# Fewer small VectorE operations in routing and list updates, and a changed instruction plan, in a recurrence followed by a mixture of experts

## The chip, the cores and the metric

The kernel runs on one core of one Trainium2 chip. The metric is the device time of one execution in microseconds: 506.29 us as the median of three runs (505.67 to 507.88). Engines are named as the profile names them: PE (TensorE matmuls), PEld (its weight loads), DVE (VectorE), ACT (ScalarE), POOL (GpSimd), SP (SyncE, which issues DMAs). L1247 is line 1247 of the kernel before.

## The reference, cut to what matters

```
x, f_logit: (4, 5056, 256) f32          # 20224 tokens of 256 values
f = lb + (1 - lb) * sigmoid(f_logit);  h_t = f_t * h_(t-1) + (1 - f_t) * x_t     # along each of 4 sequences
y = all h_t, as 20224 rows
logits = cos(y, expert_emb) / tau       # 8 experts, norms with + 1e-6
e = argmax(logits);  g = softmax(logits)[e]
out[row] = g * (relu(y[row] @ w1[e]) @ w2[e])        # w1: 256 x 1024, w2: 1024 x 256 per expert
```

## The kernel before, in words

**Routing.** The tokens go through in 40 chunks of 512 (the last is half). For each chunk PE transposes the gate input (`F_`, L667) and x (`X_`, L701) into eight [128, 512] banks of PSUM, ACT makes the gates (L678, L684), DVE multiplies (L709) and scans along time (L725). ACT squares the result (L737). From chunk 12 on ACT also writes a bf16 copy `hbf` (L743), which two transposing DMAs bring into token order (`Yt`); before that PE does it (L761). Two chunks make a group (22 groups; the first and last two have one chunk). Per group PE computes logits and squared norms (L819, L823), and DVE finds the best expert of every token, its slot, and its gate (`route_`, `gate_`: some two dozen operations on 8 to 64 columns). POOL then scatters the group's rows, 128 at a time, into a scratch tensor in DRAM that is sorted by expert (L1015, 158 scatters).

**List updates.** After 11 of the groups `update_` turns the counts per expert into a list of tiles of 256 rows of one expert: for each tile of the list the row at which it starts and the place of its expert's weights in SBUF (`tbl`).

**Expert tiles.** SP reads the start of a tile from `tbl` and loads its rows transposed from the scratch (`ys`, L1207), after all scatters of the groups that the list covers. PE runs 16 matmuls of the first layer (L1247), ACT and DVE apply relu (L1265, L1270), PE runs 16 matmuls of the second layer (L1284), ACT and DVE scale by the gate into `osb` (L1299, L1303), and POOL scatters two times 128 rows to the output (L1309). Of 86 tiles that may be needed 83 run always; the last three are skipped when the list is empty there. The weights of all experts (16 DMAs of POOL with a cast, L647) have to be in SBUF before the first tile.

**What sets the order.** `Prog.op` records every operation with what it reads, writes and costs, and `Prog.schedule` replays the engines with these costs, always giving an engine the waiting operation of the lowest `prio`, and writes a fixed order for each of the five engines and the bank of each PSUM use. The priority is the chunk for routing, 10000 + j for tile j, and -1 (ahead of everything) for a tile's evictions and output scatters. `SHADOW` and `PACE` are constants of this replay: a paced scatter on POOL gets a wait for the last PE step that ends at least `PACE` ns before the scatter's planned start.

Of the kernel before, what the change touches and what calls it, by code (L numbers as in the profile page):

```python
# [34 lines left out]
class Prog:  # L35
# [8 lines left out]
    SHADOW = 2500  # L44
    DMA_FIX = 1900
    PACE = 900.0
    DMA_RATE = 400.0

# [65 lines left out]

    def schedule(self, first, caps):
# [24 lines left out]
        bus, scat = 0.0, -1e9  # L140
# [7 lines left out]
        def lag(d):  # L148
            return d.end + self.LAT[d.eng] + self.PAD

# [5 lines left out]
        while True:  # L156
# [16 lines left out]
            if avail[e]:  # L173
                p, i, o = heapq.heappop(avail[e])
            else:
                t, p, i, o = heapq.heappop(wait[e])
            new = [h for h in o.hold if h.b is None]
# [19 lines left out]
            if o.dma is not None:  # L197
                bus = max(bus, free[e]) + o.nbytes / self.DMA_RATE
                o.end = max(bus, free[e]) + self.DMA_FIX
            else:  # L200
                o.end = free[e] + self.LAG[e]
                if e == "pe":
                    o.end = max(o.end, scat + self.SHADOW)
            if e == "pe" and not o.quiet:
                steps.append((free[e], o))
            if e == "pool" and o.dma is not None:
                scat = s
# [121 lines left out]
def bass_hgrn_recurrence__then__cosine_router_kernel(  # L329
# [20 lines left out]
    T = 256  # L350
# [17 lines left out]
    with ExitStack() as es:  # L368
# [19 lines left out]
        base17 = sb("base17", [P, 17])  # L388
        ex17 = sb("ex17", [P, 17])
# [30 lines left out]
        nr3 = [sb(f"nr3{q}", [P, 16]) for q in range(R2)]  # L420
        rs = [sb(f"rs{q}", [P, 16]) for q in range(R2)]
# [4 lines left out]
        NU = 12  # L426
        cnt = [sb(f"cnt{q}", [P, 8]) for q in range(2)]
        qn = [sb(f"qn{q}", [P, 8]) for q in range(2)]
        seg = sb("seg", [P, 16])
        cum = [sb(f"cum{q}", [P, 17]) for q in range(2)]  # L430
        cmp_ = sb("cmp", [P, 18])
        val = sb("val", [P, 17])
        t17 = sb("t17", [P, 17])
        t17b = sb("t17b", [P, 17])
        acc = [sb(f"acc{q}", [P, 2]) for q in range(2)]
        dac = sb("dac", [P, 2])
# [11 lines left out]
        NO = 4  # L448
# [3 lines left out]


        def pool(fn, cost=400, **k):
            return op("pool", fn, cost, **k)
# [12 lines left out]


# [21 lines left out]

        load(0)
        sp(lambda e: e.dma_start(embt[:], moe_expert_emb[:]), 8192, "ld0", w=["embt"])
# [13 lines left out]
        def iota(dst, pattern, base=0, mult=0, w=()):  # L507
# [3 lines left out]

        pool(lambda e: e.memset(ident[:], 0.0), w=["ident"])
# [10 lines left out]
            2, r=["lb0", "lb1"], w=["cs0"],  # L523
# [3 lines left out]
            2, r=["lb0", "lb1"], w=["cs1"],  # L527
# [13 lines left out]
        pool(lambda e: e.memset(onesb[:], 1.0), w=["onesb"])  # L541
# [10 lines left out]
        def late_constants():  # L552
            iota(iscr[:, 0:1], [[0, 1]], mult=1, w=["iscr"])
            pool(lambda e: e.tensor_copy(iop[:], iscr[:, 0:1]), r=["iscr"], w=["iop"])
            iota(iscr[:, 0:16], [[0, 2], [1, 8]], w=["iscr"])
            pool(
                lambda e: e.tensor_scalar(
                    ex17[:, 0:16], iscr[:, 0:16], float(2 * WE), 0.0, op0=ALU.mult, op1=ALU.add
                ),
                r=["iscr"], w=["ex17"],  # L560
            )
            pool(lambda e: e.memset(ex17[:, 16:17], 0.0), w=["ex17"])

            iota(iscr[:, 0:16], [[0, 2], [CB, 8]], w=["iscr"])
            pool(lambda e: e.tensor_copy(base17[:, 0:16], iscr[:, 0:16]), r=["iscr"], w=["base17"])
            pool(
                lambda e: e.tensor_scalar(
                    base17[:, 16:17], iop[:], -1.0, float(NULLROW // T), op0=ALU.mult, op1=ALU.add
                ),
                r=["iop"], w=["base17"],  # L570
# [3 lines left out]
                    nio[:], base17[:, 0:8], float(T), 0.0, op0=ALU.mult, op1=ALU.add  # L574
                ),
                r=["base17"], w=["nio"],
            )
            pool(lambda e: e.memset(nulr[:], 0.0), w=["nulr"])
# [6 lines left out]
            pool(lambda e: e.memset(acc[0][:], 0.0), w=[("acc", 0)])  # L585
            pool(lambda e: e.memset(qn[0][:], 0.0), w=[("qn", 0)])
            pool(lambda e: e.memset(cum[0][:], 0.0), w=[("cum", 0)])
            pool(lambda e: e.memset(seg[:], 1.0), w=["seg"])
# [12 lines left out]
        ]  # L601
        ew = lambda i: embw[:, D + i : D + i + 1]
# [3 lines left out]
        dve(lambda e: e.reciprocal(ew(2), ew(1)), 1, r=["ew1"], w=["ew2"])  # L606
        dve(lambda e: e.tensor_tensor(ew(3), ew(0), ew(2), ALU.mult), 1, r=["ew0", "ew2"], w=["ew3"])
        dve(lambda e: e.tensor_tensor(ew(4), ew(1), ew(3), ALU.add), 1, r=["ew1", "ew3"], w=["ew4"])
        dve(
            lambda e: e.tensor_scalar(ew(5), ew(4), 0.5, 1e-6, op0=ALU.mult, op1=ALU.add),  # L610
            1, r=["ew4"], w=["ew5"],
        )
# [20 lines left out]
        )  # L633


        def wload(i, c):
# [6 lines left out]
            else:  # L643
# [3 lines left out]
                "pool", lambda e: e.dma_start(dst, src), 1000, w=[("w", i)], dma=f"w{i}",  # L647
# [84 lines left out]
        def Y_(c):  # L732
# [8 lines left out]
            if c >= CT and nb == 4:  # L741
# [12 lines left out]
                return  # L754
            for hf in range(nb // 2):
# [23 lines left out]
                )  # L779

# [141 lines left out]
        def gate_(bi):  # L922
# [502 lines left out]
```

## Time and profile before

| | |
|---|---|
| median of 3 runs | 506.29 us |
| the profiled execution: its own time, its span | 503.07 us, 500.9 us |
| PE busy | 449.8 us, 90% |
| PEld busy | 383.7 us, 77% |
| DVE busy | 371.5 us, 74% |
| POOL busy | 337.1 us, 67% |
| ACT busy | 328.1 us, 65% |
| DMA queues q1 (SP's), q0 (POOL's) | 47.2% and 30.9% of 16 engines |
| TensorE clock granted, mean of the span | 0.971 |

Busy shares are means over two very different stages: routing with tiles between its chunks, until about 297 us, and tiles alone after it. They are read stage by stage. An instruction's duration reaches past the start of the next one on the same engine, so the cost of a small one is the distance between starts, not its duration. [...]

### The profile page before, as it was taken

Reading aid. Unit: us, or ns where it says so; the run is one execution under the profiler, and the core shown is the slowest. Engines: PE = TensorE matmul, PEld = TensorE weight load, DVE = VectorE, ACT = ScalarE, POOL = GpSimd, SP = SyncE. Lnnn points to the kernel's source line nnn. Section 1 sums busy time; section 2 is a strip of 40 time slices with the busy share of each in tenths; the row PEclk is TensorE's granted clock in tenths of the full one; section 3 lists DMA queues with packets and bytes.
Section 4 is the critical chain, followed back from the end, with each engine's and each line's share of the span. In section 5 each row is a group of like instructions: output and inputs, shape, how many; then the busy total and the mean of one; then the engine's idle time right before and its main releaser. Section 6 shows DMA issues by size and latency. Waiting matters only on the chain.

```text
span 500.9 us, 12508 instructions
## 1 busy us (share of the span) xinstructions
PE 449.8 (90%) x4009; PEld 383.7 (77%) x4009; DVE 371.5 (74%) x1202; ACT 328.1 (65%) x549; POOL 337.1 (67%) x404
## 2 busy tenths in 40 slices
PE   4878786587898999999799999999999999999994
PEld 3556564565787877877677688999999999999993
DVE  6799999576998999999899997454545545455552
ACT  6789887466787988988798844444445444454442
POOL 5144376775677677777777777777777777755565
PEclk9989989598998999999999999999999999999999
DMA  8999999789999999999998544656554456645411
GB/s 264 318 299 322 316 314 296 165 193 282 245 241 275 303 262 283 244 297 288 268 306 182 129 109 128 173 131 135 127 139 125 114 129 140 157 120 116 117 34 42
DMA packets 127584, 101.77 MB, mean 203 GB/s; under 512 B 104532, under 2 KB 106591, under 8 KB 127520
## 3 DMA queue, kind: packets, MB, share of 16 engines
q1 hardware_dynamic: 111104, 60.70, 47.2%
q0 software_dynamic: 16416, 40.27, 30.9%
q8 instruction: 34, 0.56, 0.5%
q14 instruction: 30, 0.25, 0.2%
HBM read 58.38 MB, written 34.01 MB: 184 GB/s over the span
## 4 chain that ended last, share of the span: by engine, by line
PE 57%; DVE 19%; DMA 10%; ACT 8%; issue 5%; SPq 1%; POOL 1%; ACTq 0%
PE bank L1247 23%; PE bank L1284 22%; DMA Yt<-hbf 6%; DVE hb L725 5%; PE bank L819 4%; PE bank L667 3%; DVE bank L709 3%; PE bank L701 3%; DVE hT L1270 3%; ACT fg L684 2%; DMA fin<-in_f_logit_dram 2%; ACT th L678 2%; DVE osb L1303 1%; DMA XsScratch<-Yt,sli 1%; ACT sq L737 1%
## 5 line engine op out<-in xcount | busy, mean ns | idle before, releaser
L1309 POOL DMA_INDIRECT out_dram<-osb,xm x166 | 164.6, 991 | 67.2 <-issue 30.5
L1015 POOL DMA_INDIRECT XsScratch<-Yt,sli x158 | 152.2, 963 | 58.9 <-issue 25.4
L1247 PE MATMUL bank<-ys,wall 128*128 128x256 bf16 x1328 | 167.1, 276 | 7.3 <-DMA ys<-XsScratch 5.0
L1284 PE MATMUL bank<-wall,hT 128*128 x1328 | 165.5, 273 | 3.9 <-ACT hT L1265 3.4
L1270 DVE TENSOR_SCALAR hT<-bank 128x512 bf16<-128x512 f32 x166 | 112.7, 685 | 74.9 <-PE bank L1247 72.0
L1247 PEld LDWEIGHTS bank<-ys,wall 128*128 x1328 | 149.1, 144 | 13.4 <-issue 5.6
L1284 PEld LDWEIGHTS bank<-wall,hT 128*128 128x128 bf16 x1328 | 128.5, 98 | 23.0 <-ACT hT L1265 4.2
L1265 ACT ACTIVATE hT<-bank 128x512 bf16<-128x512 f32 x166 | 98.1, 595 | 69.8 <-PE bank L1247 67.9
L725 DVE TENSOR_TENSOR_SCAN hb<-fg,hb,bank 128x512 f32<-128x512 f32 (+4 forms) x78 | 96.4, 1239 | 0.2
L1299 ACT ACTIVATE osb<-bank,xm 128x256 f32<-128x256 f32 x83 | 39.1, 471 | 47.8 <-PE bank L1284 42.3
L701 PE MATMUL bank<-ident,xin 128*128 128x128 f32 x316 | 53.3, 295 | 12.8 <-ACT fg L684 10.4
L684 ACT ACTIVATE fg<-th,cs 128x512 f32<-128x512 f32 (+1 forms) x80 | 64.0, 810 | 1.1
L1303 DVE TENSOR_SCALAR osb<-bank,xm 128x256 f32<-128x256 f32 x83 | 39.7, 478 | 31.8 <-ACT osb L1299 25.2
L709 DVE SCALAR_TENSOR_TENSOR bank<-fg,bank 128x512 f32<-128x512 f32 (+1 forms) x80 | 54.7, 686 | 7.3 <-PE bank L701 5.8
L667 PE MATMUL bank<-ident,fin 128*128 128x128 f32 x316 | 51.9, 294 | 6.4 <-DMA fin<-in_f_logit_dram 5.5
L701 PEld LDWEIGHTS bank<-ident,xin 128*128 128x128 f32 x316 | 38.2, 149 | 23.3 <-ACT fg L684 17.0
L678 ACT ACTIVATE th<-bank 128x512 f32<-128x512 f32 (+1 forms) x80 | 45.7, 587 | 8.0 <-PE bank L667 7.8
L667 PEld LDWEIGHTS bank<-ident,fin 128*128 128x128 f32 x316 | 40.0, 153 | 14.4 <-issue 7.0
L737 ACT ACTIVATE sq<-hb 128x1024 f32<-128x1024 f32 (+1 forms) x40 | 41.8, 1045 | 13.1 <-DVE hb L725 13.0
L819 PE MATMUL bank<-hb,eT 128*8 128x512 f32 (+1 forms) x160 | 41.8, 601 | 6.5 <-ACT th L678 3.3
L823 PE MATMUL bank<-sq,onesf 128*1 128x512 f32 (+1 forms) x160 | 41.7, 600 | 0.0
L743 ACT ACTIVATE hbf<-hb 128x1024 bf16<-128x1024 f32 x27 | 28.3, 1050 | 9.7 <-DMA Yt<-hbf 9.7
(114 smaller groups left out, 301.3 us busy)
## 6 DMA issues: line engine op xcount, KB each, us to landing
fin<-in_f_logit_dram SPq DMA_DIRECT2D x39, 512.0 KB
xin<-in_x_dram SPq DMA_DIRECT2D x39, 512.0 KB
wall<-in_moe_w_dram POOLq DMA_DIRECT2D x16, 512.0 KB, 10.0
out_dram<-osb,xm POOLq DMA_INDIRECT x166
XsScratch<-Yt,sli POOLq DMA_INDIRECT x158
ys<-XsScratch SPq DMA_TRANSPOSE x83
xm<-XsScratch SPq DMA_DIRECT2D x83, 2.0 KB
XsScratch<-nulr SPq DMA_DIRECT2D x8, 136.0 KB
```

The source lines that it names most:

```text
L667: i = e.transpose(bank[h.b][:, b : nb * P : nb], fin[q][:, b, dh * P : (dh + 1) * P], ident[:],)
L684: lambda e, dh=dh: e.activation(fg[c % 2][:, dh, 0:n], th[dh][:, 0:n], AF.Identity, bias=cs[:, dh, 0:1], scale=cs[:, dh, 1:2],),
L701: i = e.transpose(bank[h.b][:, b : nb * P : nb], xin[q][:, b, dh * P : (dh + 1) * P], ident[:],)
L709: lambda e, dh=dh, h=h: e.scalar_tensor_tensor(out=bank[h.b][:, 0:n], in0=fg[c % 2][:, dh, 0:n], scalar=1.0, in1=bank[h.b][:, 0:n], op0=AL ...
L725: lambda e, dh=dh, s0=s0, s1=s1, init=init, h=h: e.tensor_tensor_scan(hb[c % NH][:, dh, s0:s1], fg[c % 2][:, dh, s0:s1], bank[h.b][:, s0:s ...
L819: i = e.matmul(bank[hl.b][32 * k_ : 32 * k_ + 8, 0:n], eT[:, kt, :], hb[c % NH][:, kt, 0:n], start=(kt == 0), stop=(kt == DT - 1),)
L1015: lambda e, j=o + j, i=o + k_ * 4 + b: e.indirect_dma_start(out=Xs[:, :], out_offset=bass.IndirectOffsetOnAxis(ap=sli[y][:, j : j + 1], axis=0
L1247: i = e.matmul(bank[hh[f // 2].b][:, (f % 2) * T : (f % 2 + 1) * T], wall[:, bass.ds(a1[j][(4 * mp + f) * DT + kt] - WA - WREV, 2 * FT * P ...
L1265: lambda e, o=o, h=h: e.activation(o, bank[h.b][:], AF.Relu), 512,
L1270: lambda e, o=o, h=h: e.tensor_scalar(o, bank[h.b][:], 0.0, None, op0=ALU.max),
L1284: i = e.matmul(po(s), hT[qh][:, kf, s * P : (s + 1) * P], wall[:, bass.ds(a2[j][kf] - WA, 2 * D)].bitcast(BF16), start=(kf == 0 and s == 0 ...
L1309: lambda e, s=s: e.indirect_dma_start(out=out[:, :], out_offset=bass.IndirectOffsetOnAxis(ap=xm[qx][:, s, 1:2], axis=0), in_=osb[qo][:, s, :],
```

## The change

It rewrites two blocks of small DVE operations, changes the planner's constants and rules, and adds matmuls of ones.

- **List update.** The list entry of a tile is a sum over experts. Before, the update computed the segments, their running sum, two comparisons' difference, and two masked sums (17 operations, 22 in the last update). Now the running ends of segments come from one scan over a ring of counts, each segment adds a difference (`step`) where its end is at or below the tile's number, and one reduction continues the sum of the last update: 6 operations, and 12 in the last. The rounding of counts to whole tiles moves into a second small matmul.
- **Gate.** The inverse root takes 10 operations instead of 13 (`root`); the norm of the expert table uses `root` on DVE too, 6 operations more there, instead of a Sqrt on ACT.
- **Planner.** `SHADOW` is gone, `PACE` is 0, a POOL operation counts as 250 instead of 400 ns and a weight load as 700 instead of 1000. DVE may wait up to 250 ns for an urgent operation ahead of a long one. Output scatters of tile j rank at 10 + j/2 among the chunks, so between the scatters of routing, not ahead of them. The PE transposes of L761 rank 0.4 chunks later.
- **Fillers.** Where the plan has PE idle for over 900 ns, it inserts matmuls of ones (512 columns) into a free bank: 88 of them.
- **Buffers and end.** `osb` has 6 buffers instead of 4; in the last tile that always runs the two output halves are computed one after the other in banks of their own.

```diff
-    SHADOW = 2500
-    PACE = 900.0
+    PACE = 0.0
+    UNIT = 215.0
+    IDLE = 900.0
+    REST = 350.0
+    COLD = 12000.0
...
+            gap = s - free[e]
+            if e == "pe" and not o.late and gap > self.IDLE:
...
+                    n = int((s - a - self.REST) / (self.UNIT * (2 if s < self.COLD else 1)))
+                    if n > 0:
+                        f = self.filler(q, n)
...
-                if e == "pe":
-                    o.end = max(o.end, scat + self.SHADOW)
...
-        NO = 4
+        NO = 6
...
-        def pool(fn, cost=400, **k):
+        def warm(e, q, n):
+            for _ in range(n):
+                i = e.matmul(
+                    bank[q][:].rearrange("p (a b) -> p a b", a=4), onesb[:],
+                    onesb[:].unsqueeze(1).to_broadcast([P, 4, P]), start=True, stop=True,
+                )
+            return i
...
+        def pool(fn, cost=250, **k):
...
+        def root(n_, y_, t_, u_, v_, kn, ky, kt, ku, kv, cols):
...
         load(0)
-        sp(lambda e: e.dma_start(embt[:], moe_expert_emb[:]), 8192, "ld0", w=["embt"])
...
-        act(lambda e: e.activation(ew(1), ew(0), AF.Sqrt), 1300, r=["ew0"], w=["ew1"])
...
+        root(ew(0), ew(1), ew(2), ew(3), ew(4), ["ew0"], "ew1", "ew2", "ew3", "ew4", 1)
...
+            def total(e):
+                e.matmul(bank[h.b][:, 0:8], oneb[:], fin_oh[:, 64:72], start=True, stop=False)
+                return e.matmul(bank[h.b][:, 0:8], onesb[:], halfb[:], start=False, stop=True)
...
+            dve(
+                lambda e: e.scalar_tensor_tensor(
+                    out=ring[:, at + 8 : at + 16], in0=bank[h.b][:, 0:8], scalar=MAGIC,
+                    in1=basem[:], op0=ALU.add, op1=ALU.subtract,
+                ),
...
+                lambda e: e.scalar_tensor_tensor(
+                    out=part_[a][:, :, 16 - ns : 16],
+                    in0=ends[:, at : at + ns].unsqueeze(1).to_broadcast([P, 2, ns]),
+                    scalar=iop[:, 0:1], in1=step[:, :, 0:ns], op0=ALU.is_le, op1=ALU.mult,
+                ),
...
+                lambda e: e.tensor_reduce(
+                    part_[b][:, :, 16], part_[a][:, :, 16 - ns : 17], AX.X, ALU.add
+                ),
...
-        OUTP = lambda p: -1.0
+        OUTP = lambda p: 10 + (p - 10000) * 0.5
...
+            split = j == NM - 1
+            ho = [Hold("o"), Hold("o")] if split else [Hold("o")] * 2
...
-                sc.paced = True
+                sc.paced = j < NM - 4
```

The third list update on DVE, between a gate (`nr`, `rs`, `df`) and the scans of the chunk after it (`hb`); first as it stood, from its first operation on:

```order
L1043 TENSOR_SCALAR qn1<-bank6 128x8
L950 TENSOR_TENSOR nr31<-nr31,nrm1 128x8
L1057 TENSOR_SCALAR qn1<-qn1 128x8
L952 SCALAR_TENSOR_TENSOR nr21<-nr31,nr21 128x8
L1061 TENSOR_SCALAR qn1<-qn1 128x8
L958 SCALAR_TENSOR_TENSOR nr31<-nrm1,nr21 128x8
L1065 TENSOR_TENSOR seg<-qn1,qn0 128x8
L964 TENSOR_SCALAR nr21<-nr31 128x8
L1076 SCALAR_TENSOR_TENSOR cum1<-seg,cum0 128x8
L968 RECIPROCAL rs1<-nr21 128x8
L1084 TENSOR_SCALAR cmp<-cum1,iop 128x9
L973 TENSOR_TENSOR df1<-df1,rs1 128x64
```

The same place on DVE in the changed kernel, where `ring` to `part` are the list update and L806 is the scan:

```order
L1095 SCALAR_TENSOR_TENSOR ring<-bank4,basem 128x8
L806 SCALAR_TENSOR_TENSOR hb1<-fg0,hb0,bank5 128x512
L541 TENSOR_TENSOR nr41<-nr31,nr21 128x8
L1116 SCALAR_TENSOR_TENSOR ends<-ring,ends 128x8
L1123 TENSOR_TENSOR step<-ring 128x8
L543 TENSOR_SCALAR nr51<-nr41 128x8
L790 SCALAR_TENSOR_TENSOR bank2<-fg0,bank2 128x512
L546 TENSOR_TENSOR nr41<-nr41,nr51 128x8
L1130 SCALAR_TENSOR_TENSOR part0<-ends,iop,step 128x2x8
L806 SCALAR_TENSOR_TENSOR hb1<-fg0,hb0,bank2 128x512
L548 SCALAR_TENSOR_TENSOR nr31<-nr41,nr31 128x8
L1138 TENSOR_REDUCE part1<-part0 128x2
```

Five of the six operations of the update stand in these twelve rows, where before the first twelve held six of seventeen.

PE around the first expert tile (L1247), in the kernel before; 14 chunks have had both transposes by then:

```order
L900 MATMUL bank<-oh,onesb 128x64
L701 MATMUL bank<-ident,xin 128x128 x4
L667 MATMUL bank<-ident,fin 128x128 x4
L701 MATMUL bank<-ident,xin 128x128 x4
L667 MATMUL bank<-ident,fin 128x128 x4
L1247 MATMUL bank<-ys,wall 128x256 x16
L701 MATMUL bank<-ident,xin 128x128 x4
L667 MATMUL bank<-ident,fin 128x128 x4
```

PE around the first expert tile (now L1267) in the changed kernel; L494 are the fillers, L782 and L748 the transposes of x and of the gate input, L924 that of the logits:

```order
L906 MATMUL bank<-sq,onesf 1x512
L494 MATMUL bank<-onesb 128x512 x3
L782 MATMUL bank<-ident,xin 128x128 x4
L924 MATMUL bank<-ident,lgS 128x98 x4
L782 MATMUL bank<-ident,xin 128x128 x4
L494 MATMUL bank<-onesb 128x512 x4
L1267 MATMUL bank<-ys,wall 128x256 x16
L748 MATMUL bank<-ident,fin 128x128 x8
```

The first tile stands behind 18 chunks instead of 14. Of the 88 fillers 84 stand ahead of it. The matmul of the last list update stands inside the first layer of the 26th tile before, and behind that of the 27th's first half now.

POOL from the 13th weight load (L647) to the output scatters of the second tile (L1309), in the kernel before:

```order
L647 DMA wall<-in_moe_w_dram 128x2x1024
L1015 DMA XsScratch<-Yt,sli 164096x136 x4
L647 DMA wall<-in_moe_w_dram 128x2048
L1001 IOTA Yt 128x8
L1015 DMA XsScratch<-Yt,sli 164096x136 x8
L1001 IOTA Yt 128x8
L1015 DMA XsScratch<-Yt,sli 164096x136 x8
L1001 IOTA Yt 128x8
L1015 DMA XsScratch<-Yt,sli 164096x136
L1309 DMA out_dram<-osb,xm 20224x256 x2
L1015 DMA XsScratch<-Yt,sli 164096x136 x3
L1309 DMA out_dram<-osb,xm 20224x256 x2
```

POOL from the last weight loads (now L728) to the output scatters of the second tile (L1337) in the changed kernel, where L1066 are routing's scatters:

```order
L728 DMA wall<-in_moe_w_dram 128x2x1024
L1066 DMA XsScratch<-Yt,sli 164096x136 x2
L1052 IOTA Yt 128x8
L1066 DMA XsScratch<-Yt,sli 164096x136 x2
L728 DMA wall<-in_moe_w_dram 128x2048
L1066 DMA XsScratch<-Yt,sli 164096x136 x6
L1052 IOTA Yt 128x8
L1066 DMA XsScratch<-Yt,sli 164096x136 x8
L1052 IOTA Yt 128x8
L1066 DMA XsScratch<-Yt,sli 164096x136 x3
L1337 DMA out_dram<-osb,xm 20224x256 x2
L1066 DMA XsScratch<-Yt,sli 164096x136 x5
```

Before, 24 routing scatters stood ahead of the last weight load and 41 ahead of the first output; now 34 and 51. The last routing scatter stood behind the outputs of 56 tiles and now stands behind those of 58 and a half. On SP the first load of a tile stood behind the chunk loads of 16 gate inputs, and now stands behind 17.

## Rows read from the trace of the kernel before

**Rows 1.** Stages: window, length, busy PE, PEld, DVE, ACT, POOL, clock, DMA, GB/s.
```profile
0.00:94.00 94.00, 66.17 (x519) 48.46 (x520) 81.26 (x296) 73.05 (x116) 47.48 (x94) 0.92 1.01 293
94.00:125.00 31.00, 25.96 (x202) 20.17 (x202) 20.84 (x56) 20.05 (x31) 20.45 (x24) 0.85 0.97 229
125.00:297.00 172.00, 160.99 (x1494) 129.68 (x1493) 164.54 (x636) 141.45 (x234) 127.03 (x140) 0.99 1.01 247
297.00:494.00 197.00, 196.64 (x1800) 185.42 (x1798) 104.41 (x216) 93.06 (x169) 138.28 (x145) 1.00 0.49 123
494.00:500.90 6.90, 0.00 (x0) 0.00 (x0) 0.48 (x1) 0.47 (x1) 3.83 (x4) 0.88 0.16 52
```

**Rows 2.** Chain of waits: start, length, what; two tiles late in the span.
```profile
361.22 3.49 PE bank L1247 x32
364.71 3.49 PE bank L1284 x32
```

**Rows 3.** Second-layer matmuls until 297 us: PE, PEld busy (count), clock, DMA, GB/s.
```profile
0.00:297.00 297.00, 56.10 (x424) 40.19 (x424) 0.95 1.00 260
```

**Rows 4.** DVE in order of time: start, length, operation; small operations.
```profile
40.41 0.20 DVE L850 TENSOR_REDUCE rmax<-bank 128x8 f32<-128x64 f32 x1
...
41.95 0.69 DVE L709 SCALAR_TENSOR_TENSOR bank<-fg,bank 128x512 f32<-128x512 f32 x1
...
46.71 0.16 DVE L950 TENSOR_TENSOR nr<-nr,nrm 128x8 f32<-128x8 f32 x1
46.79 0.69 DVE L709 SCALAR_TENSOR_TENSOR bank<-fg,bank 128x512 f32<-128x512 f32 x1
...
53.95 0.17 DVE L950 TENSOR_TENSOR nr<-nr,nrm 128x8 f32<-128x8 f32 x1
54.15 0.17 DVE L952 SCALAR_TENSOR_TENSOR nr<-nr 128x8 f32<-128x8 f32 x1
```

**Rows 5.** Scans in two stages: window, length, busy DVE (count), clock, DMA, GB/s.
```profile
0.00:94.00 94.00, 35.63 (x30) 0.92 1.01 293
94.00:297.00 203.00, 65.73 (x56) 0.97 1.00 244
```

**Rows 6.** The page's DMA issues: loads of the gate input, KB of one.
```profile
fin<-in_f_logit_dram SPq DMA_DIRECT2D x39, 512.0 KB
```

**Rows 7.** First tile, chain of waits: start, length, what.
```profile
93.86 3.60 PE bank L1247 x16
```

**Rows 8.** Stages by DMA: window, length, busy engines, clock, DMA share, GB/s.
```profile
12.50:87.50 75.00, 59.27 (x489) 42.55 (x490) 68.86 (x271) 62.46 (x102) 35.26 (x47) 0.95 1.06 311
87.50:112.50 25.00, 18.21 (x133) 14.78 (x132) 16.37 (x33) 14.21 (x23) 18.50 (x21) 0.75 0.78 178
112.50:275.00 162.50, 148.86 (x1376) 120.05 (x1374) 151.44 (x542) 136.04 (x220) 117.36 (x130) 0.98 1.08 268
```

**Rows 9.** POOL in order of time: start, length, operation.
```profile
84.50 0.59 POOL L647 DMA_DIRECT2D wall<-in_moe_w_dram  x1
85.08 0.17 POOL L1001 IOTA Yt<- 128x8 int32 x1
86.06 1.00 POOL L1015 DMA_INDIRECT XsScratch<-Yt,sli  x1 [0.81 <-DVE nr L952]
87.37 0.96 POOL L1015 DMA_INDIRECT XsScratch<-Yt,sli  x1 [0.30 <-issue]
88.63 0.96 POOL L1015 DMA_INDIRECT XsScratch<-Yt,sli  x1 [0.30 <-issue]
...
203.50 1.00 POOL L1309 DMA_INDIRECT out_dram<-osb,xm  x1 [0.30 <-DVE nr L952]
204.80 1.00 POOL L1309 DMA_INDIRECT out_dram<-osb,xm  x1 [0.31 <-issue]
```

**Rows 10.** Waits of SP's and POOL's DMA issue: engine, line, releaser, us, times, longest.
```profile
SPq L306 <- DMA XsScratch<-Yt,sli: 9.7, 1, 9.7
POOL wall L647 <- DMA wall<-in_moe_w_dram: 34.5, 9, 8.3
```

More of the change, by code (lines that the diff above doesn't have):

```diff
@@ L113, in op, with filler @@
         return o
+    def filler(self, q, n):
+        f = Op()
+        f.eng, f.dma, f.nbytes, f.cost = "pe", None, 0, n * self.UNIT
+        f.val, f.know, f.used, f.tag = 0, None, False, ""
+        f.prio, f.idx, f.quiet, f.late, f.paced, f.hold = -9, len(self.ops), True, False, False, ()
+        f.deps, f.order = [self.warm_on], []
+        f.fn = lambda e: self.warm(e, q, n)
+        self.ops.append(f)
+        return f
     def schedule(self, first, caps):
@@ L149, in lag, with ready_at @@
             return d.end + self.LAT[d.eng] + self.PAD
+        def ready_at(d):
+            return lag(d) if hasattr(d, "end") else None
         def unpark(t):
@@ L172, in schedule @@
             s, e = best
-            if avail[e]:
+            soon = None
+            if e == "dve" and avail[e] and avail[e][0][2].cost > 400:
+                soon = min(
+                    (w for w in wait[e] if w[0] <= s + 250 and w[1] < avail[e][0][0] and w[1] <= 1),
+                    default=None, key=lambda w: w[:3],
+                )
+            if soon is not None:
+                wait[e].remove(soon)
+                heapq.heapify(wait[e])
+                s, p, i, o = soon
+            elif avail[e]:
                 p, i, o = heapq.heappop(avail[e])
@@ L176, in schedule @@
                 t, p, i, o = heapq.heappop(wait[e])
+            gap = s - free[e]
+            if e == "pe" and not o.late and gap > self.IDLE:
+                room = [(t, q) for q, t in enumerate(frees) if t is not None and t <= s - self.IDLE]
+                if room and ready_at(self.warm_on) is not None:
+                    t, q = min(room)
+                    a = max(t, free[e], ready_at(self.warm_on))
+                    n = int((s - a - self.REST) / (self.UNIT * (2 if s < self.COLD else 1)))
+                    if n > 0:
+                        f = self.filler(q, n)
+                        f.start = a
+                        free[e] = a + n * self.UNIT * (2 if s < self.COLD else 1)
+                        f.end = free[e] + self.LAG[e]
+                        if banks[q][1].eng != e:
+                            f.deps.append(banks[q][1])
+                        banks[q][1], frees[q] = f, free[e]
+                        out.append(f)
             new = [h for h in o.hold if h.b is None]
@@ L420, in bass_hgrn_recurrence__then__cosine_router_kernel @@
         nr3 = [sb(f"nr3{q}", [P, 16]) for q in range(R2)]
+        nr4 = [sb(f"nr4{q}", [P, 16]) for q in range(R2)]
+        nr5 = [sb(f"nr5{q}", [P, 16]) for q in range(R2)]
         rs = [sb(f"rs{q}", [P, 16]) for q in range(R2)]
@@ L425, in bass_hgrn_recurrence__then__cosine_router_kernel @@
         sli = [sb(f"sli{q}", [P, 16], I32) for q in range(NY)]
[L426 to L436, printed above, removed]
+        step = sb("step", [P, 2, 16])
+        part_ = [sb(f"part{q}", [P, 2, 17]) for q in range(2)]
+        tblf = sb("tblf", [P, 2])
+        over = sb("over", [P, 1])
         tbl = [sb(f"tbl{q}", [P, 2], I32) for q in range(NU)]
@@ L1192, in addresses @@
             ]
+        NM = NT - 3
         a1, a2 = {}, {}
```

311 lines of the change are left out of this document (136 added, 175 removed).

## The prediction

> **What bounds the kernel now.** I read the stages first, then the chain of waits, then DVE, POOL and the DMA shares of the routing stage. The stages [rows 1] fall in two. From 297 to 494 us PE is busy for 196.64 of 197.0 us at full clock: tiles alone, nothing to win. Two tiles take 6.98 us there [rows 2], one 3.49 us. By 297 us 424 of the 1328 second-layer matmuls have run [rows 3], which at 16 a tile is 26.5 tiles; the other 56.5 at 3.49 are the 197 us. So the end is the moment T at which 26.5 tiles and all routing are done, plus 197.0, plus 6.9 for the last evictions and scatters [rows 1], plus 2.2 between the span and the execution's own time. Before, T is 297.
>
> Up to T no engine is full on the average, but several nearly are by turns: from 125 to 297 us DVE has 164.54 of 172 and PE 160.99, and POOL issues scatters at a pitch of 1.26 (routing) and 1.30 us (output) with only its 0.30 us gap between them [rows 9]. From 12.5 to 87.5 us the DMA engines stand at a share of 1.06 [rows 8]: loads of chunks and weights at once. Between 87.5 and 112.5 us all sag (DMA 0.78, DVE 16.37 of 25). There SP sat 9.7 us on a wait for scatters [rows 10] before it could load the first tile, with chunk loads queued behind it, and the first tile began at 93.86 [rows 7] at half clock (16 matmuls in 3.60 instead of 1.75 us).
>
> **The change part by part.**
>
> DVE loses 66 operations in the gates (22 times 3) and 120 in the updates (192 become 72), and gains 6 for the expert table: 180 fewer. The twelve operations from 40.41 to 41.95 stand 0.128 us apart [rows 4]. One squeezed between long operations costs 0.08 (46.71 to 46.79), one that waits for the one before it 0.20 (53.95 to 54.15). So 180 are worth 23 us, between 14 and 36; I take 23, since most stand interleaved with others. DVE has 266.6 us of work before 297 us (the first three stages); 243.6 stay.
>
> A page of the Trainium skill, "Perfetto Trace Analysis", section Optimizing Scalar/DVE Operations, gives some 60 ns of engine time as the overhead of a DVE operation on SBUF. By it 180 operations would be an estimated 11 us. The distances between starts here, 0.08 to 0.20 us, are above that, so the rows decide. The sum stands without it.
>
> PE is not shortened by the edits, but by the clock. Mean granted clocks of 0.92, 0.85 and 0.99 (times at 1.2 instead of 2.4 GHz) cost about 0.08 of 66.17, 0.15 of 25.96 and 0.01 of 160.99: 10.8 us. The fillers are to keep the clock up. Busy PE before T is 253.1, so 242.3 at full clock: 92.6 for 26.5 tiles, 149.7 for 40 chunks, 3.74 us a chunk. A filler of 512 columns is two of a tile's matmuls of 256, so 2 x 3.49/32, about 0.22 us: 88 cost 19 us. 84 stand before the first tile, where PE is idle anyway: 18 chunks at 3.74 are 67 us, with the fillers 86, and that stage lasts over 100. So I cost them at nothing; if their cover were gone, at most 19.
>
> The first tile is moved from behind 14 to behind 18 chunks. DVE could be there early: 30 of 86 scans ran beside 81 us of busy DVE before [rows 5]; 36 for 18 chunks would be 97, less 18/40 of the 23, plus the 13 us it idles in that stage, gives 100 us. But the DMA engines are full. Four more chunks are four times two loads of 512 KB [rows 6], 4.2 MB, which at the 311 GB/s of the saturated stage [rows 8] is 13.5 us, so that weights and 18 chunks are in at 93.9 + 13.5 = 107.4 us. I take 107.4; bounds 100 and 114 (with the transposing DMAs of chunks 12 to 17 beside them).
>
> From the first tile to T, 22 chunks and 26.5 tiles remain: PE 22 x 3.74 + 92.6 = 174.9 us; DVE 243.6 less the first 87 = 157; POOL 77 routing and 52 output scatters at 1.26 and 1.30, about 165 with its iotas uncounted. Now PE is the longest, and it stands first. T = 107.4 + 174.9 = 282.3, down by 14.7. PE would need no idle time for that, but 3.74 also holds PE's own transposes of the first 12 chunks, which this stage doesn't have; I let the two cancel. Bounds for this stage: 166 (those transposes counted off) and 186 (PE no denser than the 94% of 125 to 297 before).
>
> Smaller parts: the two table loads around the Sqrt, the changed waiting of DVE for evictions, six `osb` buffers and a later rank of outputs. The first lies in a stage that DMA bounds now, the second is inside DVE's slack of 18 us, the others move POOL's work and are priced as a rival. The split last tile can bring its first half forward by under 0.9 us; taken as 0 to -1.
>
> Sum: 282.3 + 197.0 + 6.9 + 2.2 = 488.4 on the scale of the profiled execution (503.07). The median before lies 3.2 higher, so **492 us** against 506.29. With both stages at their bounds, T is 266 to 300; the likely part of that is 275 to 290, times of 485 to 499.
>
> **Rivals.**
>
> *DMA sets the pace (499 us).* Shares of 1.06 and 1.08 [rows 8] may be the ceiling. Then no load comes earlier than its bytes allow, and only the sag of 0.78 over 25 us can be refilled: (1.07 - 0.78) x 25 = 7 us, so 506.3 - 7 = 499. For it: the shares, and POOL's 34.5 us of waiting for weights [rows 10]. Against: my stage after 107 us asks for a chunk every 175/22 = 7.95 us, where the one before got 26 in 203 us [rows 5], one every 7.8.
> The Trainium skill, "DMA: Bandwidth & Descriptors", section Issuing engines are not separate DMA queues, says that DMAs of all issuing engines interleave on the same 16 engines. By that rule chunk loads that come faster take from the weights; the 1.06 with both queues at work agrees, and this is the rival's mechanism.
>
> *POOL sets the end (slower, 514 us).* POOL must issue 124 routing and 118 output scatters after the last weight load until the outputs of 58 tiles: 124 x 1.26 + 118 x 1.30 = 310, with some 14 iotas that each cost about 0.7 (from the load's end at 85.09 to 86.06, less the usual 0.30) [rows 9] 320 us. The last weight load was issued at 84.5; if now at 90, POOL is there at 410. PE reaches tile 65, which needs the buffer of tile 59, at 282 + 38.5 x 3.49 = 416.7. That is 7 us of margin. With `PACE` at 0 each scatter waits for a PE step planned to end just when it starts, so any lateness of PE reaches POOL. If that adds 0.12 us to the pitch of the 242 scatters, POOL is 29 us later, 22 of it on the end: 492 + 22 = 514. It decides from +0.03 us on, and makes the kernel slower than before from about +0.10, or from a last weight load 24 us later still. For it: POOL ran at its pitch without slack already. Against: it has ten more scatters behind it at that point of its order than before, and six buffers.
>
> *Routing's gain shows fully (478 us).* If weights land by 100 us and PE runs at 97%, T is about 268. For it: DVE's 100 us and PE's bound of 166. Against: the DMA share.
>
> *The change doesn't do what it says:* fillers that stand where PE is really late delay it and the clock falls nevertheless. It keeps at most the 3.9 us of clock of the stage from 94 to 125 and some fillers, 3 to 8 us, so times of 495 to 500; it sits in the first rival's range.
>
> **How the numbers follow.** Forecast (485 to 499) 0.53; DMA or fillers (495 to 505) 0.20; full gain (about 478) 0.08; POOL (506 to 525) 0.13; nothing seen 0.06. 0.5%, about what a measurement of this kernel can tell from no change, is 2.5 us: faster is below 503.8, slower above 508.8. Faster: 0.53 + 0.08 + most of the 0.20, 0.79. Slower: 0.12 of POOL's 0.13 and none else. The same: 0.09. The range is 477 to 508; the likeliest case alone 485 to 499.
>
> **What would show it.** In the changed profile the stage of tiles alone should again be PE at over 99%, and start near 282 us. The first tile should start at 104 to 112 us, at full clock, with no long wait of SP for scatters before it. DVE's busy time up to T should be about 23 us lower. POOL's pitch should stay at 1.26 to 1.30 with gaps of 0.30. I am wrong in the first part if the first tile starts after 118, in the second if PE idles over 12 us between it and the tile stage, and altogether if PE idles in the tile stage for output buffers.

## The result: 498 us, 1.6 to 2.3% faster

The changed kernel takes 498.44 us in the median (496.00 to 498.94, four runs) where the kernel before takes 506.28 beside it: 0.984 of it, with an interval of 0.980 to 0.988. Run again in another session it takes 494.83 against 508.13, 0.977 (0.971 to 0.982). The forecast of 492 was 0.972.

The profiled execution takes 498.83 us with a span of 497.0. Line numbers have moved: L782 holds the transposes of x (L701 before), L1267 and L1312 the two layers (L1247, L1284), L1285 the eviction of the hidden layer by ACT (L1265), L824 the bf16 copy `hbf` of the later chunks (L743), L829 the DMAs that transpose it (L748), L1227 a tile's load (L1207), L494 the fillers.

The stages first, cut at the first tile and where the tiles alone begin (window, length, busy PE, PEld, DVE, ACT, POOL, with counts, clock, DMA share, GB/s; the share is the sum of the packets' times over that of 16 engines, so above 1 packets overlap):

```profile
0.00:111.80 111.80, 94.38 (x712) 62.59 (x713) 93.04 (x302) 83.98 (x133) 63.89 (x113) 0.97 1.03 289
111.80:295.40 183.60, 171.26 (x1603) 141.15 (x1602) 164.65 (x548) 148.11 (x244) 128.75 (x143) 0.98 0.98 243
295.40:491.10 195.70, 195.61 (x1791) 184.98 (x1790) 99.86 (x174) 93.69 (x169) 143.36 (x149) 1.00 0.51 125
491.10:497.00 5.90, 0.80 (x8) 0.47 (x5) 0.48 (x1) 0.47 (x1) 2.96 (x3) 0.82 0.16 51
```

Against [rows 1]: tiles alone are again a full PE (195.61 of 195.70), the end is 1.0 us shorter. T is 295.4 instead of 297, and the sum had 282.3. PE idles 17.4 us before the first tile and 12.3 us from there to T.

The chain of waits up to the first tile (start, length, what):

```profile
75.61 9.37 DMA XsScratch<-Yt,sli
85.08 0.80 SPq L1225
86.31 1.64 SPq L1227
...
93.27 1.41 SPq L1227
...
94.78 6.36 DMA xin<-in_x_dram
101.28 1.08 PE bank L782 x4
...
105.43 4.15 DMA xin<-in_x_dram
...
111.12 0.86 PE bank L494 x4
111.98 1.09 PE bank L1267 x10
```

The wait for scatters is still there. SP loads three tiles (86.31 to 94.67) before it comes to chunk 16's x, which PE then waits for. The hole that stood ahead of the first tile [rows 7] stands behind chunk 15 now. The first tile does start at full clock.

The wait of ACT and the two of PE between 112 and 290 us that matter most, then SP from 75 to 112 and POOL's weight loads in the whole span (engine, line, releaser: us in all, times, longest):

```profile
ACT hbf L824 <- DMA Yt<-hbf: 12.4, 8, 3.4
PE bank L1312 <- ACT hT L1285: 7.7, 4, 3.3
PE bank L782 <- ACT fg L765: 4.1, 2, 2.2
SPq L345 <- DMA XsScratch<-Yt,sli: 5.7, 1, 5.7
POOL wall L728 <- DMA wall<-in_moe_w_dram: 19.6, 6, 6.2
```

PE's idle time there is nearly all behind ACT (11.8 of 12.3 us), and ACT waits for a free `hbf` buffer until the transposing DMAs have read it; the evictions that PE needs stand behind the copy in ACT's order. The longest such place, in the chain of waits; PE had idled 3.31 us at its end:

```profile
138.25 6.82 DMA Yt<-hbf
...
145.09 1.06 ACT hbf L824
146.15 0.48 ACT th L759
146.63 0.49 ACT hT L1285
...
147.17 1.89 PE bank L1312 x8
```

Five of PE's eight waits there, 9.8 us in all, end in this way, 1.6 to 2.7 us after a copy that had waited starts. Against [rows 10], SP's wait went from 9.7 to 5.7 and POOL's from 34.5 to 19.6.

The page's first row, and POOL in order of time:

```profile
PE 462.0 (93%) x4108; PEld 389.2 (78%) x4108; DVE 358.0 (72%) x1022; ACT 326.3 (66%) x546; POOL 339.0 (68%) x406
```

```profile
92.91 0.99 POOL L1066 DMA_INDIRECT XsScratch<-Yt,sli  x1 [0.30 <-issue]
94.21 0.96 POOL L1066 DMA_INDIRECT XsScratch<-Yt,sli  x1 [0.30 <-issue]
...
205.85 1.01 POOL L1337 DMA_INDIRECT out_dram<-osb,xm  x1 [0.20 <-issue]
207.16 1.00 POOL L1337 DMA_INDIRECT out_dram<-osb,xm  x1 [0.30 <-DVE nr L529]
```

DVE has 1022 instructions instead of 1202, but only 13.5 us less work (371.5 before). POOL's pitch is 1.26 to 1.31 where nothing else holds it, with gaps of 0.20 to 0.30, as in [rows 9].

### The profile page after: what moved, and what is told of

Read it like the earlier page. It is cut to its first block, busy times and chain, and to the rows that moved or that the text cites. A ratio compares the mean times of both kernels' runs of the same rounds, so it can differ in the third digit from the quotient of the medians.

```text
span 497.0 us, 12465 instructions
## 1 busy us (share of the span) xinstructions
PE 462.0 (93%) x4108; PEld 389.2 (78%) x4108; DVE 358.0 (72%) x1022; ACT 326.3 (66%) x546; POOL 339.0 (68%) x406
## 4 chain that ended last, share of the span: by engine, by line
PE 69%; DMA 12%; ACT 8%; SPq 4%; DVE 3%; issue 2%; POOL 0%; POOLq 0%; DVEq 0%
PE bank L1312 27%; PE bank L1267 26%; PE bank L782 5%; DMA Yt<-hbf 5%; DMA xin<-in_x_dram 5%; PE bank L902 4%; PE bank L748 3%; DMA XsScratch<-Yt,sli 2%; SPq L1227 2%; ACT fg L765 2%; ACT hbf L824 2%; ACT th L759 1%; ACT sq L818 1%; PE bank L843 1%; DVE hb L806 1%
## 5 line engine op out<-in xcount | busy, mean ns | idle before, releaser
L1337 POOL DMA_INDIRECT out_dram<-osb,xm x166 | 164.9, 993 | 64.5 <-issue 28.4
L1066 POOL DMA_INDIRECT XsScratch<-Yt,sli x158 | 152.7, 967 | 66.2 <-issue 24.7
L1312 PE MATMUL bank<-wall,hT 128*128 x1328 | 174.8, 274 | 8.0 <-ACT hT L1285 7.7
L1267 PE MATMUL bank<-ys,wall 128*128 128x256 bf16 x1328 | 172.3, 273 | 0.3 <-issue 0.2
L1290 DVE TENSOR_SCALAR hT<-bank 128x512 bf16<-128x512 f32 x166 | 113.6, 685 | 62.3 <-PE bank L1267 61.7
L1285 ACT ACTIVATE hT<-bank 128x512 bf16<-128x512 f32 x166 | 98.7, 595 | 90.9 <-PE bank L1267 90.6
L1267 PEld LDWEIGHTS bank<-ys,wall 128*128 x1328 | 150.2, 144 | 4.3 <-issue 1.3
L1312 PEld LDWEIGHTS bank<-wall,hT 128*128 128x128 bf16 x1328 | 129.0, 98 | 28.9 <-ACT hT L1285 9.2
L806 DVE TENSOR_TENSOR_SCAN hb<-fg,hb,bank 128x512 f32<-128x512 f32 (+4 forms) x78 | 95.9, 1234 | 0.2
L782 PE MATMUL bank<-ident,xin 128*128 128x128 f32 x316 | 52.4, 291 | 16.7 <-DMA xin<-in_x_dram 10.3
L782 PEld LDWEIGHTS bank<-ident,xin 128*128 128x128 f32 x316 | 37.6, 148 | 30.0 <-ACT fg L765 14.1
L759 ACT ACTIVATE th<-bank 128x512 f32<-128x512 f32 (+1 forms) x80 | 46.1, 589 | 21.5 <-PE bank L748 12.3
L748 PE MATMUL bank<-ident,fin 128*128 128x128 f32 x316 | 49.8, 287 | 1.2 <-DVE embw L541 1.2
L748 PEld LDWEIGHTS bank<-ident,fin 128*128 128x128 f32 x316 | 38.6, 148 | 5.9 <-DVE embw L541 2.1
L824 ACT ACTIVATE hbf<-hb 128x1024 bf16<-128x1024 f32 x27 | 28.4, 1052 | 12.4 <-DMA Yt<-hbf 12.4
## 6 DMA issues: line engine op xcount, KB each, us to landing
wall<-in_moe_w_dram POOLq DMA_DIRECT2D x16, 512.0 KB, 10.8
```

The costliest lines, as they stand in the source:

```text
L748: i = e.transpose(bank[h.b][:, b : nb * P : nb], fin[q][:, b, dh * P : (dh + 1) * P], ident[:],)
L782: i = e.transpose(bank[h.b][:, b : nb * P : nb], xin[q][:, b, dh * P : (dh + 1) * P], ident[:],)
L806: lambda e, dh=dh, s0=s0, s1=s1, init=init, h=h: e.tensor_tensor_scan(hb[c % NH][:, dh, s0:s1], fg[c % 2][:, dh, s0:s1], bank[h.b][:, s0:s ...
L1066: lambda e, j=o + j, i=o + k_ * 4 + b: e.indirect_dma_start(out=Xs[:, :], out_offset=bass.IndirectOffsetOnAxis(ap=sli[y][:, j : j + 1], axis=0
L1267: i = e.matmul(bank[hh[f // 2].b][:, (f % 2) * T : (f % 2 + 1) * T], wall[:, bass.ds(a1[j][(4 * mp + f) * DT + kt] - WA - WREV, 2 * FT * P ...
L1285: lambda e, o=o, h=h: e.activation(o, bank[h.b][:], AF.Relu), 512,
```

## Experiments

Theory A was that the expected gain went into two waits in in-order queues: SP's list ahead of the first tile, and ACT's wait for a copy buffer. B held that the DVE operations themselves give nothing, C that the DMA engines set the pace.

**e1, the old operations in the new plan.** Edit: `update_`, the root in `gate_`, and their constants of before put back.

> The changed kernel with the 21-operation list update and the longer gate of before put back (186 small VectorE operations more); the planner, its fillers, the six output buffers and the ranks stay as changed. The plan is made anew, and it puts the first tile behind 16 chunks instead of 18. Theory A (what VectorE saved went into two waits in queues, so its operations are worth little): VectorE's busy time up to the tile stage goes up by some 10 us, the time by 2 to 5 us, 500 to 504. The price of my prediction (0.128 us an operation, all of it on the path): 510 or more. Rival B (operations worth nothing, the gain is the plan and the fillers): 498 to 499.

Measured: 501.12 us, 0.987 of before (0.983 to 0.991). The page's first row:

```profile
PE 460.6 (92%) x4081; PEld 385.6 (77%) x4081; DVE 370.5 (74%) x1208; ACT 324.8 (65%) x546; POOL 338.7 (68%) x404
```

186 operations cost DVE 12.5 us (370.5 against 358.0), 0.067 each, and the time rises by 0.3 to 1.0% against the two measurements of the changed kernel, of which the intervals can't tell the 0.3 from nothing. Theory A's size; the price of 0.128 is refuted.

**e2, the new operations in the old plan.** Edit: the same pieces the other way round, in the kernel before.

> The kernel before with only the new list update and the new gate; its planner with SHADOW 2500, PACE 900 and no fillers, four output buffers and the old ranks stay. Theory A: the wait of SyncE for scatters ahead of the first tile and the half clock stay, and 2 to 5 us are won: 501 to 504. Prediction's price: 492 to 496. Rival B: 506, no change.

Measured: 499.34 us, 0.985 (0.981 to 0.990), more than theory A expected. Its DVE has 356.3 us of work, 15.2 less for 186 operations: 0.082 each. Its profiled execution, 501.71, is the slowest of its six, and that of before (503.07) is quicker than all 23 runs of it beside e2, so the traces don't show where the 7.7 us came from. Operations alone give 1.5%, the plan and fillers alone (e1) 1.3%, both together 1.6 to 2.3%: in the first session the gains overlap, in the second they may just as well add up. B is refuted. Which of the planner's rules, buffers and ranks give the 1.3% was not taken apart, the fillers (e3) excepted.

**e3, no fillers.**

```diff
-            if e == "pe" and not o.late and gap > self.IDLE:
+            if e == "pe" and not o.late and gap > 1e9:
```

> The changed kernel without its 88 filler matmuls; every other instruction of every engine stands in the same order. Theory A: PE has slack up to the first tile, since that stage waits for loads and scatters, so the fillers are worth what the clock gives: with a granted clock of 0.92 instead of 0.97 in that stage the end moves by 0 to 4 us, 498 to 503. Rival B (the gain is the fillers): 504 to 507. Rival C (fillers stand in the way of late work): 494 to 497.

Measured: 491.77 us, 0.970 (0.965 to 0.975). Faster without them than any of the three had it. The stages, and ACT's wait from 112 to 290 us:

```profile
0.00:112.90 112.90, 79.22 (x629) 57.49 (x630) 92.75 (x301) 84.41 (x133) 63.26 (x113) 0.94 1.03 288
112.90:288.30 175.40, 168.88 (x1602) 139.14 (x1601) 164.31 (x548) 147.82 (x244) 127.97 (x142) 1.00 1.01 253
```

```profile
ACT hbf L824 <- DMA Yt<-hbf: 7.4, 6, 2.6
```

Up to the first tile the fillers do what they are for, a clock of 0.97 instead of 0.94; the first tile starts at 112.8 without them and at 111.8 with them (110.7 in e10, below, so 1 us is what two runs of one kernel differ by). Behind it the stage lasts 175.4 instead of 183.6 us, PE idles 6.5 instead of 12.3, and ACT waits 7.4 instead of 12.4, in the same order of instructions.

**e10, the changed kernel again**, since it had not run beside e3.

> The changed kernel itself, fillers and all, on one chip with e9. It has not run beside e3, so that the 6.7 us between them rest on two sessions. If the fillers cost what they seem to, it is again 0.980 to 0.988 of before; if e3's gain is one of the session, 0.968 to 0.975.

Measured: 494.83 us, 0.977 (0.971 to 0.982), between the two answers. Two windows, and ACT's wait:

```profile
0.00:110.70 110.70, 94.08 (x712) 62.37 (x713) 93.00 (x302) 84.02 (x133) 63.86 (x113) 0.97 1.03 293
110.70:290.70 180.00, 170.11 (x1603) 139.92 (x1602) 164.74 (x548) 147.83 (x244) 128.73 (x142) 0.99 1.02 247
```

```profile
ACT hbf L824 <- DMA Yt<-hbf: 10.2, 7, 4.0
```

Against e3's 0.970 that is 0.6% more, against the first session 1.4%; the interval overlaps e3's. No run shows the fillers earning anything over the whole span; that they cost some 3 to 7 us is likely. How the two that stand between the first tile and T, or the 84 ahead of it, would lengthen ACT's wait is open, and so is how much of 12.4, 10.2 and 7.4 is one execution differing from another.

**e4, scatters planned to land 7 us later.**

```diff
                 o.end = max(bus, free[e]) + self.DMA_FIX
+                if e == "pool" and o.nbytes == 67584:
+                    o.end += 7000.0
```

> The changed kernel with one number of the plan altered: the planner takes the routing scatters to land 7 us later than it did, so SyncE's list has the loads of chunk 17 and the f load of chunk 17 and the transposes of chunk 12 ahead of the first tile's load. Theory A: the hole of 10 us in the chunks before the first tile closes, chunk 17 is transposed by 104 instead of 110, the tile stage starts 4 to 8 us earlier: 490 to 495. Rival C (the DMA engines are at their ceiling there, so a load that comes earlier delays another): 497 to 500. Rival D (tiles that come later in the plan leave PE short of work between chunks): 500 to 504.

Measured: 506.34 us, 0.999 (0.996 to 1.003). Loads of chunks 16 and 17 now stand ahead of the first tile's, and the hole has moved behind chunk 17: PE idles 10.3 us there. SP in order of time (start, length, operation):

```profile
83.85 7.95 SPq L831 DMA_TRANSPOSE Yt<-hbf  x2
91.90 0.55 SPq L571 DMA_DIRECT2D xin<-in_x_dram  x1
...
98.47 9.42 SPq L1229 DMA_TRANSPOSE ys<-XsScratch  x1
108.09 0.42 SPq L1234 DMA_DIRECT2D xm<-XsScratch  x1
```

SP waits for no semaphore here, yet one tile's load holds it for 9.42 us and two transposes of a copy for 7.95, where the changed kernel's tile loads took 1.21 to 1.64. The chain of waits through the hole:

```profile
85.30 19.56 DMA Yt<-hbf
...
104.88 1.06 ACT hbf L826
105.93 0.95 ACT sq L820
...
106.93 3.59 PE bank L904 x8
```

A transposing DMA sent at 85.3 lands 19.56 us later, ACT idles 10.52 us for the buffer that it reads, and PE waits for the operation behind ACT's copy: the hole is now theory A's other wait. For SP's list theory A is wrong in this stage: this order of it doesn't close the hole. The stage behind it became longer as well.

**e7, e8 and e11, SyncE's costs in the plan** as the traces show them, all three without fillers; e8 with three copy buffers, e11 on top of e9 below. The edit of the costs, with what stands between left out:

```diff
-            return op("sp", fn, 60, dma=dma, nbytes=nbytes, **k)
+            return op("sp", fn, 450, dma=dma, nbytes=nbytes, **k)
...
-                    sp(
+                    op(
+                        "sp",
...
-                        230000, f"yt{y}_{k_}", r=[("hbf", c % NHF)], w=[("Yt", y, k_, dh)],
+                        1250, nbytes=230000, dma=f"yt{y}_{k_}", r=[("hbf", c % NHF)], w=[("Yt", y, k_, dh)],
...
-            lo = op("sp", ld, 700, r=rd, w=[("ys", qy)], dma=f"xs{qy}", nbytes=230000)
-            op("sp", ldm, 100, r=rd, w=[("xm", qx)], dma=f"xm{qx}", nbytes=16384, order=[lo])
+            lo = op("sp", ld, 1700, r=rd, w=[("ys", qy)], dma=f"xs{qy}", nbytes=230000)
+            op("sp", ldm, 450, r=rd, w=[("xm", qx)], dma=f"xm{qx}", nbytes=16384, order=[lo])
```

> The changed kernel without fillers, and with SyncE's costs in the plan as the traces show them: 1.25 us for each transposing DMA (the plan had 0.06), 1.7 us for a tile's load with its table read (0.7), 0.45 for an ordinary load (0.06). The plan then puts one tile load and not three ahead of chunk 16's load, and the first tile behind 17 chunks. Theory A (SyncE's list is what makes the hole of 10 us ahead of the first tile): the hole shrinks by 4 to 8 us, and the time against e3's 491.8 to 484 to 488. Rival (the DMA engines are full there, or the wait moves to the next load): 490 to 494. A plan with longer SyncE costs that starves PE of chunks later: over 495.

> As e7_sync_costs, and three copy buffers as in e6. If both waits are separate, the gains add: 480 to 485. If only one of them is on the path, the time is that of the better of e7 and e6 less e3's gain, 485 to 490.

> e9 (no fillers, chunks 12 to 17 transposed on TensorE) with SyncE's costs in the plan as the traces show them (1.25 us a transposing DMA, 1.7 a tile's load, 0.45 an ordinary load). One tile load instead of three then stands ahead of chunk 16's load, and no transposing DMA of a copy up to chunk 22's load. Theory A (the order of SyncE's list makes the hole of 8 us that e9 still has, and e7 kept it only because the transposing DMAs held SyncE): chunk 16 is transposed by 98 instead of 105, the first tile starts at 103 to 107, and the end comes 2 to 6 us before e9's: 480 to 484 where before takes 507. Rival C (the DMA engines are full up to the last weight, whatever the order): the hole only moves to another load, 485 to 488. The later part keeps its 3 us of idle in both.

Measured: 585.71, 584.28 and 582.04 us, beside 591 to 592 for the kernel before: 0.987 (0.982 to 0.993), 0.988 (0.982 to 0.994), 0.984 (0.980 to 0.988). These three, e5, e6 and e12 ran on two chips on which every kernel, before's too, takes some 85 us longer, nearly all of it behind the first tile; their times answer none of the expectations. The stage ahead of it can still be read, in e8:

```profile
88.00 0.50 SPq L569 DMA_DIRECT2D xin<-in_x_dram  x1
...
89.65 10.79 SPq L830 DMA_TRANSPOSE Yt<-hbf  x2
101.61 1.22 SPq L1228 DMA_TRANSPOSE ys<-XsScratch  x1
```

Chunk 16's x is sent for at 88.0 instead of 94.8, and then two transposes hold SP for 10.79 us. The first tile starts at 106.0, behind 17 chunks, the earliest of the new plans; in e7 it starts at 113.6, with two transposes holding SP for 13.06 us, and in e11 at 114.6. Whether e8's start would reach the end on a chip like those of the other runs is open.

**e5, fillers in the first 60 us only; e6, three copy buffers.** Edits: `s < 60000` in the condition of e3; `NHF = 3`.

> The changed kernel with only the 41 fillers that the plan puts in its first 60 us; the other 47, in the stage of weights and scatters up to the first tile, two at 173 us and two at the end, are left out. All other instructions stand in the same order. If the late fillers do the harm that e3 showed (they stand where PE is late, or make PE run in another rhythm against the DMA engines), the time is that of e3, 490 to 494; if the early ones do it, that of the changed kernel, 497 to 500; if both do, about 495.

> The changed kernel, fillers and all, with three instead of two buffers for the bf16 copies that the transposing DMAs read; the plan is made anew. Theory A (ScalarE's wait for a free copy buffer, 12.4 us from 110 to 300 us, holds the evictions queued behind it and costs PE its idle time there): the wait falls under 3 us, PE's idle from the first tile to the tile stage from 12 to about 6 us, 491 to 495. Rival (the wait only moves: the DMAs have the same work and the matmuls or scatters wait for them instead): 497 to 500.

Measured: 584.17 us, 0.988 (0.983 to 0.993), and 583.29 us, 0.985 (0.981 to 0.990), on the first of the chips just named. Inconclusive: in e5, with two buffers, ACT doesn't wait for `hbf` at all, so a third one has nothing to remove there.

**e9, chunks 12 to 17 transposed on PE** (no fillers).

```diff
-        CT = 12
+        CT = 18
```

> The changed kernel without fillers, with chunks 12 to 17 transposed on TensorE, as chunks 0 to 11 are, instead of by transposing DMAs (CT 18 instead of 12): 12 such DMAs fewer, all of them in the stretch from 83 to 118 us, where SyncE was held up to 13 us in issuing one and where no order of its list has closed the hole. The first tile stands behind 17 chunks. Theory C' (the DMA engines are at their ceiling there, and a transposing DMA costs them more than its bytes): the hole of 10 to 15 us between two chunks falls to under 6 us, the first tile starts at 104 to 108 instead of 112.9 and the end moves by 4 to 8 us against e3: 484 to 488 where before takes 507. Theory A (the tile loads' wait for scatters in SyncE's list makes the hole): it stays, 490 to 493. Rival (TensorE and ScalarE pay for the transposes what the DMAs save): 492 to 497.

Measured: 485.92 us, 0.958 (0.954 to 0.962), the fastest. Stages, then ACT's wait (112 to 290 us) and PE's (84 to 112 us):

```profile
0.00:110.00 110.00, 78.84 (x648) 57.67 (x649) 92.19 (x297) 82.23 (x134) 61.91 (x111) 0.94 1.03 296
110.00:284.90 174.90, 171.53 (x1627) 143.23 (x1626) 164.47 (x537) 149.85 (x249) 128.81 (x142) 0.99 1.00 244
```

```profile
ACT hbf L824 <- DMA Yt<-hbf: 3.8, 1, 3.8
...
PE bank L782 <- DMA xin<-in_x_dram: 8.2, 1, 8.2
```

The size is what C' expected, but not by its way: the hole stays (8.2 us), and the tile starts at 110.0, 2.8 us before e3's but behind 17 chunks instead of 18. What fell is ACT's wait, to 3.8 us, and PE's idle time behind the first tile, to 3.4. The plan was made anew, so which part of it gained the time is not separated.

**e12, e9 with three copy buffers**, same order.

> e9 with three instead of two copy buffers; the order of every engine's instructions is e9's. ScalarE waited 3.8 us for a free copy in e9 and TensorE was idle 3.4 us between the first tile and the tile stage. Theory A: the wait goes and 0 to 3 us are won: 483 to 486. Rival (a copy made earlier only lets the next DMA queue up earlier): 486, the same.

Measured: 584.52 us, 0.989 (0.986 to 0.992) on the second such chip; inconclusive (e11, with two buffers, has no wait for `hbf` there either). What these chips do is seen in a stretch of tiles alone, first e12, then e9:

```profile
350.00:470.00 120.00, 97.55 (x844) 86.97 (x844) 46.45 (x79) 40.25 (x78) 71.03 (x75) 0.99 0.40 99
```

```profile
350.00:470.00 120.00, 120.00 (x1101) 113.78 (x1100) 61.08 (x104) 57.48 (x103) 88.29 (x93) 1.00 0.52 124
```

## Why the prediction was right in its direction, and 6 us short

Faster, and inside the range; the forecast's own range (485 to 499) held both sessions. On the scale of the profiled executions the sum was 488.4, measured is 498.83. Of the 10.4 us between them, T is 13.1 late, of which 4.4 lie ahead of the first tile and 8.7 behind it. The tail (195.7, 5.9 and 1.8 instead of 197.0, 6.9 and 2.2) gives 2.7 back. The medians differ by less, 6.4 us, since the profiled execution of before was 3.2 us quicker than its median and this one 0.4 slower.

That the direction came out is in part luck. T moved by 1.6 us in the first session's trace (297 to 295.4) and by 6.3 in the second's (290.7), where the argument had 14.7; in the first most of the 4.2 us between the two profiled executions is the tail, to which the sum had given none. The number 498 is also what two of the rivals had.

**DVE, 180 operations at 0.128 us: the term was mis-sized.** 13.5 us of busy time went in all, 0.075 each, and up to T 8.9 (266.6 to 257.7) instead of 23. e1 and e2 put one at 0.067 and 0.082. The distance between starts [rows 4] was the wrong row: at 0.20 apart (53.95 to 54.15) an operation of 0.17 us waits for the one before it, and other work can fill such waits; what went with an operation was near the 0.08 of one squeezed between long ones. It moved no number of the sum: DVE was only to be shorter than PE's 174.9 us behind the first tile, and with the measured 164.65 it is. The Trainium skill, "Perfetto Trace Analysis", section Optimizing Scalar/DVE Operations, has some 60 ns as DVE's overhead on SBUF; that agrees with 0.067 to 0.082, and I had set it aside.

**First tile at 107.4: 111.8 and 110.7, inside 100 to 114.** The mechanism, DMA, is likely by the share, but no run shows it alone: with other orders of SP's list e1, e4 and e9 start it at 108.6, 113.6 and 110.0 (behind 16, 18 and 17 chunks), and from 87.5 to 112.5 us the share, 0.78 before [rows 8], is

```profile
87.50:112.50 25.00, 16.03 (x116) 9.79 (x109) 14.33 (x53) 12.02 (x19) 15.72 (x20) 0.86 1.05 229
```

in the changed kernel. But a full share is 229 GB/s here, not the 311 with which I priced the four chunks; at 229 their 4.2 MB are 18.3 us and the tile comes at 112.2. In the changed kernel's packet records, summed by size, the 256-byte packets of transposing DMAs are 18.0 MB in 94.5 us of all 16 engines, 190 GB/s; the 4 KB packets of SP's loads get 359. Whether the size of the packets or the transposing makes the difference, no run separates. The Trainium skill, "Advanced Engine Details and Errata", section X-Bar Transpose (TRN2), says that transposing DMAs are as fast as regular ones; these records, 190 beside 359, don't bear that out here.

**The stage from the first tile to T at 174.9: 183.6 and 180.0, and 175.4 and 174.9 in e3 and e9.** PE's own work was 171.26 us, 3.6 less than priced. The step that failed was "PE would need no idle time": it idles 12.3. I had read the waits of SP and POOL [rows 10] and not ACT's, which stood in the trace of before; there, between 112 and 290 us:

```profile
ACT hbf L743 <- DMA Yt<-hbf: 7.4, 6, 3.3
112.00:290.00 178.00, 164.17 (x1511) 130.67 (x1510) 166.78 (x616) 147.51 (x241) 129.24 (x143) 0.98 1.04 256
```

In this window PE's idle time goes with ACT's wait over seven traces: 12.3 us at 12.4 of wait, 9.9 at 10.2 (e10), 6.5 at 7.4 (e3), 3.4 at 3.8 (e9), 8.8 at 7.7 (e1), 12.6 at 11.9 (e2) and 15.7 at 12.9 (e4). The kernel before is the exception, 13.8 at 7.4; its PE waited for many other things. The new plan is not what makes the wait long: e3 has its order and 7.4, e2 has the old plan and 11.9. That the wait makes the idle time is shown place by place in the changed kernel's chain, ACT's copy ahead of the eviction, and once more in e4's; what makes the wait longer or shorter is open, and the runs that would have removed it alone (e6, e12) told nothing. That e3 and e9 come so near to 174.9 is luck: 168.88 and 171.53 of work, the rest idle.

**Fillers at nothing, 10.8 us of half clock back.** They took 15.2 us of PE up to the first tile (94.38 against e3's 79.22), and PE was idle there anyway, as I said. The clock before it rose to 0.97, but that stage waits for DMA, so it was worth 1.0 or 2.1 us (112.8 against 111.8 and 110.7), hardly more than those two differ by; behind it the mean clock is 0.98 with them and 1.00 without. The cost I took as lost to the clock was mostly hidden already.

**The rivals.** DMA as the pace gave 499, which is the number measured, and by the share it is right ahead of the first tile. Behind it e3 and e9 take 175 us at a share of 1.00 to 1.01, so the 183.6 of the changed kernel at 0.98 are not the DMA engines' limit; whether the 175 are, no run shows, though in e9 PE idles only 3.4 of them. POOL as the end is refuted: pitch and gaps as before, and PE waits for nothing between 296 and 490 us. The full gain (478) no run reached; e9 comes to 485.92 with two edits that the change doesn't have. The fourth, fillers that delay PE, I had at 495 to 500; e3 speaks for a part of it.

**My own marks.** Wrong in the second part "if PE idles over 12 us" behind the first tile: 12.3, and 9.9 in the second session. The tiles alone start at 295.4 and 290.7, not near 282. "No long wait of SP for scatters" failed with 5.7 us. POOL, the clock at the first tile and the tiles alone were as told.

## What to carry to other kernels

Price a removed small operation by the busy time that goes with it, not by the distance of starts, and count it only where that engine ends last. Before counting a stage at one engine's busy time, list what every engine waits for in it, above all copies behind which evictions stand in the same queue. An idle stretch that waits for transfers was closed here neither by other orders of the same list (e4, e8) nor by keeping the clock up; e9, with 12 transposing DMAs fewer, was the fastest, though its hole stayed too.

## What the runs showed of the hardware

- Issuing a transposing DMA holds SP without a semaphore to wait for: 1.2 us at the least and 1.2 to 1.3 in the median of the changed kernel, but 9.42 for one (e4, DMA share 1.16 in that stretch) and 10.79 for two (e8, 1.18). A load of `xin` or `fin` there holds it 0.33 us at the least, 0.42 to 0.44 in the median and 1.66 at the most.
- The 21,248 packets of 8 bytes that bring the tiles' gates and row numbers (256 rows of 83 tiles) are 0.17 MB and take 12.5 us of all 16 DMA engines, an eighth of what the 256-byte packets take for 18.0 MB.
- On two of the chips, of which e12's trace shows one, PE is busy 97.55 of 120 us in tiles alone, at nearly the same clock (0.99, in e9 1.00). The idle 22.4 us stand ahead of the second layer: 16.0 waiting for ACT's eviction, which itself takes no longer, and 6.0 for issue. Gains are small there: the ratios of e5 to e8, e11 and e12 to before lie between 0.984 and 0.989.
- One number of a plan moves the end by as much as the whole change: e4, with the same work but for 12 fillers, is 1.6 to 2.3% slower than the changed kernel.
